# Moving the gate products, the key transposes and the score products to other places between the product groups of a fused attention and mixture-of-experts kernel

## The chip, the cores and the metric

The kernel runs on one core of a Trainium2 chip, as one launch. The metric is the time of that launch on the device, in microseconds. Each version is executed several times and the median counts. A profiled execution gives the trace from which the rows below come.

## The reference, cut to what matters

Three stages follow each other. Attention with 32 memory slots for each of 8 batches and 8 heads:

```python
a = softmax(phi, axis=seq)                       # 576 positions, 32 slots
k_m, v_m = a.T @ k, a.T @ v                      # per batch and head: 32 x 64
attn = softmax(scale * q @ k_m.T) @ v_m          # 576 x 64
x = attn, heads side by side                     # 4608 tokens x 512
```

Then a first feed-forward stage, `h = max(x @ w1, x @ w2, x @ w3)` (512 to 768) and `h @ w_out` (768 to 512). Then a second stage in which every token goes to the one of 8 experts with the highest `x @ w_gate`: `relu(x @ w1[e]) @ w2[e]`, times the gate's softmax value.

## The kernel before, in words

All products that carry precision are done as three products of split operands (`mm3`, L99 to L102: high by high, low by high, high by low). The kernel never forms the attention output. `u_step(b, f)` (L407) multiplies the memory values `vT` of batch b by the f-th 128 columns of the three first-stage weights, and splits the result into `u_hi` (ScalarE) and `u_lo` (VectorE). `m1_step` (L435) then multiplies u by the attention weights `at_hi`, `at_lo`. These 6 matmuls of 288 columns are one product group. The groups of one f come as two halves of the sequence by three weights (hf, i), so six groups use one u, and a batch has 36 groups. The first of three groups is copied out of PSUM by ScalarE into `hx` (L448). The second and third are folded into it by VectorE (`max`, L450), and after the third ScalarE and GpSimd make `h_hi` and `h_lo`. Then `m2_step` (L471) does the eight outputs of the batch by `wo_hi`, `wo_lo`.

PSUM has four tiles for product groups (`ps_mm`), two for u products (`ps_u`) and two for everything else (`ps_at`). `at_scores` takes both `ps_at` and both `ps_u` tiles. So TensorE can be at most four groups ahead of the engines that empty them.

Between the groups of batch b stand three other kinds of work. First, the attention of batch b + 1 (`attention`, L366): column maxima of phi, exponentials, `at_asum` (four VectorE operations), `at_km` (148 small products, L258), `at_kvT` (three transposes, L299, copied out as `kT` and `vT`), `at_scores` (64 products, L318, four VectorE transposes out of PSUM), then maxima, exponentials, sums and `at_out`. Second, the gate of batch b - 1: `gate_a` (16 products, L487), `gate_b` (five transposes and a chain of twelve small VectorE operations with one ScalarE exponential, L502, then a DMA issued by ScalarE), `gate_c` (two products and eight small VectorE operations, L535). Third, the u products: `u_step(b, 2)` to `u_step(b, 5)` are written in front of f = 1 to 4 of the same batch, and the first two u products of the next batch among its second-stage products.

Where the first two kinds go is set by a list of due times. A `Stream` holds (time, function) pairs, each product group advances its clock by 0.97, each second-stage step by 2.25, and whatever has come due is written then. `AT` (L56) is the list of the attention of batches 2 to 7, which are done in batches 1 to 6, the steady batches. Batch 1 has a list of its own, `AT1`. In the following, group n is the n-th product group of a batch. With these clocks the order before is: `gate_a` behind group 3, `gate_b` and the second u product (f = 2; counted here by its place, the first of the four in the batch) behind group 6, `gate_c` and the next u product (f = 3) behind group 12, `at_km` and u of f = 4 behind group 18, `at_kvT` behind group 19, `at_scores` behind group 22, u of f = 5 behind group 24.

TensorE's queue keeps this written order. The queues of VectorE and ScalarE don't: the framework's scheduler takes, for each engine, the earliest written operation that its own estimate calls ready, so later work can slip in front of earlier work that is still waiting. Once compiled, the order is fixed.

Of the kernel before, what the change touches and what calls it, by code (L numbers as in the profile page):

```python
# [19 lines left out]
def kernel(  # L20
# [32 lines left out]
    WARM = 17  # L53
    NRAW = 6

    AT = dict(max=1, col=4.5, sub=6.5, q=(0, 2, 3.5, 5), exp=9, asum=11, km=16.5, kvT=18, sc=20.5,  # L56
              smax=(24.5, 27), sexp=(29, 31), ssum=(34, 37), out=(41.5, 45))
    AT1 = dict(max=18, col=19, sub=20.5, q=(30, 31, 32, 33), exp=22, asum=23, km=31, kvT=33, sc=36,
               smax=(38, 39.5), sexp=(39.5, 41), ssum=(42, 44), out=(45, 47))
    XN = 256  # L60
# [65 lines left out]
    def load_phi(b, src=None):  # L126
        t = ep.tile([P, J, NCH, M], F32, tag="phi", name="phi_t")
        if src is not None:
            after(t[:, 0, 0, 0:1], src)
        nc.sync.dma_start(out=t.rearrange("p j c m -> p j (c m)"), in_=pairs(phi[b]))  # L130
        inp["phi", b] = t
# [234 lines left out]
    def attention(b):  # L366

        T = AT if b > 1 else AT1
        L = [
# [117 lines left out]
    def gate_a(b):  # L487
        gsb = mo["sy"].tile([P, S], F32, tag="gsb", name="gsb")
        st["gsb", b] = gsb
        for hf in range(2):  # L490
            ps = ps_at.tile([P, 512], F32, tag="at", name="ps_g")
            for d in range(ND):
                nc.tensor.matmul(
                    out=ps[32 * d:32 * d + 32, :HS],
                    lhsT=wg[:, d, :],
                    rhs=ys[b][:, d, hf * HS:(hf + 1) * HS],
                    start=True,
                    stop=True,
                )
            nc.scalar.activation(out=gsb[:, hf * HS:(hf + 1) * HS], in_=ps[:, :HS], func=AF.Copy)  # L500

    def gate_b(b):  # L502
        gsb = st.pop(("gsb", b))

        lg = rsmall.tile([P, NTT, E], F32, tag="glg", name="glg")
        for t0, t1 in ((0, 3), (3, NTT)):
            ps = ps_at.tile([P, 512], F32, tag="at", name="ps_l")
            for t in range(t0, t1):
                nc.tensor.transpose(ps[:, (t - t0) * P:(t - t0 + 1) * P], gsb[:, TT0[t]:TT0[t] + P], ident)
            nc.vector.tensor_reduce(  # L510
                out=lg[:, t0:t1],
                in_=ps[:, :(t1 - t0) * P].rearrange("p (t d e) -> p t e d", d=ND, e=32)[:, :, :E],
                axis=AX.X, op=ALU.add,
            )
        mx = rsmall.tile([P, NTT, 1], F32, tag="gmx", name="gmx")
        nc.vector.tensor_reduce(out=mx[:, :, 0], in_=lg, axis=AX.X, op=ALU.max)
        sh = rsmall.tile([P, NTT, E], F32, tag="gsh", name="gsh")
        nc.vector.tensor_tensor(out=sh, in0=lg, in1=mx.to_broadcast([P, NTT, E]), op=ALU.subtract)
        oh = rsmall.tile([P, NTT, E], F32, tag="goh", name="goh")
        nc.vector.scalar_tensor_tensor(out=oh, in0=sh, scalar=0.0, in1=w8, op0=ALU.is_ge, op1=ALU.mult)  # L520
        nc.scalar.activation(out=sh, in_=sh, func=AF.Exp)
        gt = gi[:, b, 0:NTT]
        ix = gi[:, b, NTT:2 * NTT]
        nc.vector.tensor_reduce(out=ix, in_=oh, axis=AX.X, op=ALU.max)
        nc.vector.tensor_tensor(out=oh, in0=w8, in1=ix.unsqueeze(2).to_broadcast([P, NTT, E]), op=ALU.is_equal)
        nc.vector.tensor_tensor(out=oh[:, NTT - 1], in0=oh[:, NTT - 1], in1=own, op=ALU.mult)
        oc = rsmall.tile([P, E], F32, tag="goc", name="goc")
        nc.vector.tensor_reduce(out=oc, in_=oh.rearrange("p t e -> p e t"), axis=AX.X, op=ALU.add)
        nc.vector.tensor_reduce(out=gt, in_=sh, axis=AX.X, op=ALU.add)
        nc.vector.tensor_scalar(out=gt, in0=gt, scalar1=EPS, scalar2=None, op0=ALU.add)  # L530
        nc.vector.reciprocal(out=gt, in_=gt)
        nc.scalar.dma_start(out=g_dram[b], in_=gi[:, b])
        st["goc", b] = oc

    def gate_c(b):  # L535
        oc = st.pop(("goc", b))
        ps = ps_at.tile([P, 512], F32, tag="at", name="ps_c")
        nc.tensor.matmul(out=ps[:, :E], lhsT=ones, rhs=oc, start=True, stop=True)
        cnt = rsmall.tile([P, E], F32, tag="cnt", name="cnt")
        nc.vector.tensor_copy(out=cnt, in_=ps[:, :E])  # L540
        cm = rsmall.tile([P, 1], F32, tag="cm", name="cm")
        nc.vector.tensor_reduce(out=cm, in_=cnt, axis=AX.X, op=ALU.max)
        ce = rsmall.tile([P, E], F32, tag="ce", name="ce")
        nc.vector.scalar_tensor_tensor(out=ce, in0=cnt, scalar=cm, in1=w8[:, 0], op0=ALU.is_equal, op1=ALU.mult)
        nc.vector.tensor_reduce(out=cm, in_=ce, axis=AX.X, op=ALU.max)

        nc.vector.scalar_tensor_tensor(
            out=scal[:, b], in0=gi[:, b, NTT:2 * NTT], scalar=cm, in1=gi[:, b, 0:NTT], op0=ALU.is_equal, op1=ALU.mult
        )

        nc.vector.tensor_scalar(out=ce, in0=w8[:, 0], scalar1=cm, scalar2=None, op0=ALU.not_equal)
        nc.vector.tensor_tensor(out=rest[:, b], in0=cnt, in1=ce, op=ALU.mult)
        nc.vector.tensor_scalar(out=e1i[0:1, b:b + 1], in0=cm[0:1], scalar1=-1.0, scalar2=float(E), op0=ALU.mult, op1=ALU.add)
# [264 lines left out]
    with ExitStack():  # L818
# [65 lines left out]
        def start_step():  # L884
            if started[0] < len(wparts):
                w_done(started[0], scored if started[0] < 8 else None)
                started[0] += 1

        for b in range(B):
            stream = Stream(attention(b + 1) if b + 1 < B else [])  # L890
            if b > 0:
                stream.add([(2, lambda: gate_a(b - 1)), (5, lambda: gate_b(b - 1)), (11.5, lambda: gate_c(b - 1))])
            else:
                done = lambda n: wdst[n][0:1, 0:1]
                stream.add([(10, lambda: load_phi(1, done(10)))])
                stream.add([(16 + i, lambda i=i: load_kv(1, i, done(13))) for i in range(2)])
                stream.add([(20 + j, lambda j=j: load_q(1, j, done(15))) for j in range(J)])
            for f in range(NF1):
                if f + 1 < NF1 and b > 0 and f > 0:
                    u_step(b, f + 1)  # L900
                if (b, f) == (B - 1, NF1 - 2):
                    early.close()
                    mo["stack"] = ExitStack()
                    mo["xp", 0] = mo["stack"].enter_context(tc.tile_pool(name="xp", bufs=1, side="right"))
                    feed = Feed(
                        [(c, 0, i) for c in "y12" for i in range(ND)]
                        + [(c, n, i) for n in range(1, B) for c in "y12" for i in range(ND)]
                        + [("1", B, i) for i in range(ND)]
                    )
                    feed.load_to(feed.AHEAD)  # L910
                    stream.add([(1 + 1.7 * i, feed.step) for i in range(3 * ND)])
                for hf in range(2):
                    for i in range(3):
                        m1_step(b, f, hf, i)
                        if b == 0 and (hf, i) in ((0, 0), (0, 2), (1, 1)):
                            start_step()
                        if b == 0 and 0 < f < NF1 - 1 and (hf, i) == (1, 0):
                            u_step(0, f + 1)
                        stream.advance(0.97)
            if b == 0:  # L920
                while started[0] < len(wparts):
                    start_step()
                start.close()
                mo["sy"] = late.enter_context(tc.tile_pool(name="sy", bufs=1))
            for hf in range(2):
                if b == 0 and hf == 0:
                    m2_by_f(b, hf, stream)
                    continue
                for d in range(ND):
                    m2_step(b, d, hf)  # L930
                    stream.advance(2.25)
                    if b + 1 < B and (hf, d) in (((0, 2), (1, 1)) if b else ((1, 0), (1, 1))):
                        u_step(b + 1, int((hf, d) == (1, 1)))
            stream.rest()
# [46 lines left out]
        for b in range(B):  # L981
            stream = Stream([])
# [75 lines left out]
```

## Time and profile before

| | us |
|---|---|
| median of 3 runs | 1015.35 |
| lowest and highest run | 1012.68, 1017.62 |
| the profiled execution's own time | 1014.16 |
| its span, first to last instruction | 1012.4 |

Some 2 us of the execution lie outside the span. Times in the rows are microseconds from the start of the span. In a timeline row the columns are start, duration, engine, line, operation, output and inputs, shape, count of merged instructions, and in brackets how long the engine had been idle and what ended that. PE is TensorE's matmuls, PEld its weight loads, DVE VectorE, ACT ScalarE, ACTq ScalarE's queue when it issues a DMA. Matmuls are pipelined, so the start of one to the start of the next is the time that counts.

### The profile page before, as it was taken

What the parts mean: (1) busy time and instruction counts of PE and PEld (TensorE: products, weight loads), DVE (VectorE), ACT (ScalarE), POOL (GpSimd) and SP (SyncE); (2) the same over time, 40 slices, a digit from 0 to 9 for tenths busy, and PEclk for the clock granted to TensorE, in tenths of its full rate; (3) what the DMA queues carried; (4) which work ended last, traced back from release to release, by engine and by line L of the source; (5) the groups of instructions that cost most, each with busy time, mean ns of one, the idle gap of its engine ahead of it and who ended that gap; (6) DMA issues with size and microseconds to landing.
All of it is one profiled execution on the core that took longest, in us unless ns stands there. A gap on an engine that the chain in (4) does not pass through costs nothing. (4 is left out here: it accounts for less than half of the span.)

```text
span 1012.4 us, 20551 instructions
## 1 busy us (share of the span) xinstructions
PE 978.7 (97%) x8306; PEld 854.6 (84%) x8306; DVE 562.1 (56%) x1289; ACT 370.5 (37%) x808; POOL 149.9 (15%) x259
## 2 busy tenths in 40 slices
PE   7888999999999999999999999999999999999996
PEld 4466788879888898988989989898989898989885
DVE  6889877473674737657165727171717171716341
ACT  2555343333433324334245415050506060604130
POOL 0000012110211102112021130202021212121110
PEclk9899999999999999999999999999999999999999
DMA  8487423132221322110117417171717161615030
GB/s 288 135 259 262 141 66 103 47 130 83 75 92 48 131 83 75 46 47 2 48 61 251 164 40 221 35 226 32 229 32 228 33 212 49 211 45 151 22 110 22
DMA packets 59107, 114.79 MB, mean 113 GB/s; under 512 B 7687, under 2 KB 20999, under 8 KB 59008
## 3 DMA queue, kind: packets, MB, share of 16 engines
q1 hardware_dynamic: 48480, 94.01, 28.5%
q0 software_dynamic: 4768, 9.94, 4.2%
q10 hardware_dynamic: 5760, 9.48, 2.5%
q8 instruction: 67, 1.10, 0.5%
q14 instruction: 32, 0.26, 0.1%
HBM read 94.00 MB, written 19.44 MB: 112 GB/s over the span
## 5 line engine op out<-in xcount | busy, mean ns | idle before, releaser
L100 PE MATMUL ps_m<-at_hi,u_hi 128*128 128x288 f32 x576 | 177.9, 310 | 6.9 <-ACT hx L448 3.2
L102 PE MATMUL ps_m<-at_hi,u_lo 128*128 128x288 f32 x576 | 170.5, 297 | 0.2 <-ACT u_lo L427 0.2
L101 PE MATMUL ps_m<-at_lo,u_hi 128*128 128x288 f32 x576 | 170.3, 296 | 0.1
L100 PE MATMUL ps_x<-yh,w1h 128*128 128x288 f32 (+1 forms) x544 | 160.3, 295 | 0.2 <-DVE xh L617 0.2
L101 PE MATMUL ps_x<-yl,w1h 128*128 128x288 f32 (+1 forms) x544 | 159.9, 294 | 0.0
L102 PE MATMUL ps_x<-yh,w1l 128*128 128x288 f32 (+1 forms) x544 | 159.8, 294 | 0.0
L97 POOL TENSOR_TENSOR h_lo<-hx,h_hi 128x288 fp32r<-128x288 f32 x84 | 72.9, 868 | 466.3 <-ACT h_hi L96 462.3
L100 PEld LDWEIGHTS ps_m<-at_hi,u_hi 128*128 128x128 f32 x576 | 108.2, 189 | 37.3 <-issue 14.2
L646 POOL DMA_DIRECT2D out_dram<-o x144 | 71.1, 500 | 346.2 <-DVE o L643 306.0
L450 DVE TENSOR_TENSOR hx<-hx,ps_m 128x288 f32<-128x288 f32 x192 | 85.5, 448 | 65.2 <-PE ps_m L102 40.9
L100 PE MATMUL ps_m<-h_hi,wo_hi 128*128 128x288 f32 x384 | 115.1, 300 | 1.9 <-DVE hx L450 1.8
L101 PE MATMUL ps_m<-h_lo,wo_hi 128*128 128x288 f32 x384 | 113.2, 295 | 0.0
L102 PE MATMUL ps_m<-h_hi,wo_lo 128*128 128x288 f32 x384 | 113.0, 295 | 0.0
L102 PEld LDWEIGHTS ps_m<-at_hi,u_lo 128*128 128x128 f32 x576 | 108.7, 189 | 1.4 <-ACT u_lo L427 0.7
L101 PEld LDWEIGHTS ps_m<-at_lo,u_hi 128*128 128x128 f32 x576 | 108.7, 189 | 1.2 <-issue 1.0
L643 DVE TENSOR_SCALAR o<-ps_x,scal 128x512 f32<-128x512 f32 x32 | 24.0, 751 | 151.6 <-PE ps_x L102 151.6
L100 PE MATMUL ps_x<-w2h,xh 128*128 128x512 f32 x272 | 107.7, 396 | 0.0
L101 PE MATMUL ps_x<-w2l,xh 128*128 128x512 f32 x272 | 107.5, 395 | 0.0
L102 PE MATMUL ps_x<-w2h,xh 128*128 128x512 f32 x272 | 107.4, 395 | 0.0
L100 PEld LDWEIGHTS ps_x<-yh,w1h 128*128 128x128 f32 x544 | 102.3, 188 | 1.5 <-DVE xh L617 0.5
L101 PEld LDWEIGHTS ps_x<-yl,w1h 128*128 128x128 f32 x544 | 102.1, 188 | 0.6 <-ACT yl L732 0.2
L102 PEld LDWEIGHTS ps_x<-yh,w1l 128*128 128x128 f32 x544 | 102.1, 188 | 0.0
(200 smaller groups left out, 1593.6 us busy)
## 6 DMA issues: line engine op xcount, KB each, us to landing
raw<-in_moe_w_dram SPq DMA_DIRECT2D x72, 512.0 KB, 4.7
raw<-y_dram SPq DMA_DIRECT2D x36, 288.0 KB, 3.1
w<-in_moe_w_dram SPq DMA_DIRECT2D x18, 512.0 KB, 5.1
kv_t<-in_k_dram SPq DMA_DIRECT2D x8, 1152.0 KB, 7.1
kv_t<-in_v_dram SPq DMA_DIRECT2D x8, 1152.0 KB, 9.8
q_t<-in_q_dram SPq DMA_DIRECT2D x32, 288.0 KB, 3.0
y_dram<-y_sb ACTq DMA_DIRECT2D x32, 288.0 KB, 2.1
out_dram<-o POOLq DMA_DIRECT2D x144, 64.0 KB, 1.9
```

Source lines behind the costliest of these rows:

```text
L97: eng.tensor_tensor(out=dst_lo, in0=src, in1=dst_hi, op=ALU.subtract)
L100: nc.tensor.matmul(out=ps, lhsT=hi_l, rhs=hi_r, start=first, stop=False)
L101: nc.tensor.matmul(out=ps, lhsT=hi_l, rhs=lo_r, start=False, stop=False)
L102: nc.tensor.matmul(out=ps, lhsT=lo_l, rhs=hi_r, start=False, stop=last)
L450: nc.vector.tensor_tensor(out=hx[0], in0=hx[0], in1=ps, op=ALU.max)
L643: nc.vector.tensor_scalar(out=o, in0=ps, scalar1=scal[:, b, t:t + 1], scalar2=None, op0=ALU.mult)
L646: nc.gpsimd.dma_start(out=out5[b, half, c], in_=o[i:i + TB])
```

## The change

It moves work between the product groups of the steady batches, and the gate's work also in batch 7. Nothing is added or removed, and no size changes.

```diff
-    AT = dict(..., km=16.5, kvT=18, sc=20.5,
-              smax=(24.5, 27), sexp=(29, 31), ssum=(34, 37), out=(41.5, 45))
+    AT = dict(..., km=16.5, kvT=23.2, sc=25.5,
+              smax=(29.5, 31.5), sexp=(33.5, 35.5), ssum=(38, 40.5), out=(44, 47))
...
-                stream.add([(2, lambda: gate_a(b - 1)), (5, lambda: gate_b(b - 1)), (11.5, lambda: gate_c(b - 1))])
+                stream.add([(5.7, lambda: gate_a(b - 1)), (11.5, lambda: gate_b(b - 1)), (23.1, lambda: gate_c(b - 1))])
```

By the clocks the new order is: `gate_a` and u of f = 2 behind group 6, `gate_b` and u of f = 3 behind group 12, `at_km` and u of f = 4 behind group 18 as before, `gate_c`, `at_kvT` and u of f = 5 behind group 24, `at_scores` behind group 27. The softmax of the scores is written later too: its last step, `at_out` for the second half, behind the sixth of the eight second-stage steps in place of the fifth. The loads of the next batch's phi, k and v are written with `at_kvT`.

## Rows read from the trace of the kernel before

**Rows 1.** The page: busy time of TensorE and others over the span.
```profile
PE 978.7 (97%) x8306; PEld 854.6 (84%) x8306; DVE 562.1 (56%) x1289; ACT 370.5 (37%) x808; POOL 149.9 (15%) x259
```
**Rows 2.** Windows view: busy time and instructions by engine, then PEclk, granted clock.
```profile
193.43:204.89 11.46, 11.36 (x103) 9.60 (x101) 10.89 (x35) 5.25 (x13) 2.52 (x3) 1.00 0.01 0
```
**Rows 3.** Waits from 125 to 500 us: total, times, longest.
```profile
PEld ps_u L414 <- DVE sc L335: 5.8, 12, 1.1
```
**Rows 4.** Timeline of PE in batch 2, around u of f = 5.
```profile
217.20 0.29 PE L102 MATMUL ps_m<-at_hi,u_lo 128*128 128x288 f32 x1
218.32 1.24 PE L414 MATMUL ps_u<-w,vT 64*32 64x384 f32 x16 [0.83 <-DVE sc L335]
219.49 0.40 PE L100 MATMUL ps_m<-at_hi,u_hi 128*128 128x288 f32 x1
```
**Rows 5.** Timeline of PE in batch 2, u of f = 4.
```profile
209.60 0.88 PE L414 MATMUL ps_u<-w,vT 64*32 64x384 f32 x16
210.40 0.40 PE L100 MATMUL ps_m<-at_hi,u_hi 128*128 128x288 f32 x1
210.64 0.29 PE L101 MATMUL ps_m<-at_lo,u_hi 128*128 128x288 f32 x1
```
**Rows 6.** Timeline of PE in batch 2, around gate_a.
```profile
188.92 0.29 PE L102 MATMUL ps_m<-at_hi,u_lo 128*128 128x288 f32 x1
189.14 1.18 PE L493 MATMUL ps_g<-y_sb,wg 128*32 128x288 f32 x16
190.25 0.40 PE L100 MATMUL ps_m<-at_hi,u_hi 128*128 128x288 f32 x1
```
**Rows 7.** Timeline of PE in batch 2, from u of f = 2 to group 18.
```profile
193.50 0.88 PE L414 MATMUL ps_u<-w,vT 64*32 64x384 f32 x16
...
198.37 0.29 PE L102 MATMUL ps_m<-at_hi,u_lo 128*128 128x288 f32 x1
198.76 0.41 PE L100 MATMUL ps_m<-at_hi,u_hi 128*128 128x288 f32 x1
...
199.89 0.88 PE L414 MATMUL ps_u<-w,vT 64*32 64x384 f32 x16
...
204.51 0.29 PE L101 MATMUL ps_m<-at_lo,u_hi 128*128 128x288 f32 x1
204.64 0.29 PE L102 MATMUL ps_m<-at_hi,u_lo 128*128 128x288 f32 x1
204.93 0.40 PE L100 MATMUL ps_m<-at_hi,u_hi 128*128 128x288 f32 x1
```
**Rows 8.** Timeline of DVE in batch 2, the same stretch and u of f = 4.
```profile
193.43 0.40 DVE L510 TENSOR_REDUCE glg<-ps_l 128x24 f32<-128x96 f32 x2
...
196.10 0.98 DVE L97 TENSOR_TENSOR u_lo<-ps_u,u_hi 128x384 fp32r<-128x384 f32 x2
196.99 1.35 DVE L243 TENSOR_TENSOR phi_t<-phi_t,ps_mb 128x1152 f32<-128x1152 f32 x1
198.26 1.59 DVE L450 TENSOR_TENSOR hx<-hx,ps_m 128x288 f32<-128x288 f32 x3
199.96 0.69 DVE L217 TENSOR_TENSOR hc<-phi_t 128x512 f32<-128x512 f32 x1
...
201.52 0.15 DVE L540 COPY cnt<-ps_c 128x8 f32<-128x8 f32 x1
...
203.57 0.21 DVE L547 SCALAR_TENSOR_TENSOR scal<-gi,cm 128x5 f32<-128x5 f32 x1
...
204.44 0.99 DVE L450 TENSOR_TENSOR hx<-hx,ps_m 128x288 f32<-128x288 f32 x2
...
211.60 1.02 DVE L97 TENSOR_TENSOR u_lo<-ps_u,u_hi 128x384 fp32r<-128x384 f32 x2 [1.48 <-ACT u_hi L96]
```
**Rows 9.** Timeline of ACT in batch 2, behind gate_b.
```profile
196.21 0.34 ACTq L532 DMA_DIRECT2D g_dram<-gi  x1
196.65 0.41 ACT L448 ACTIVATE hx<-ps_m 128x288 f32<-128x288 f32 x1 [0.46 <-DVE u_lo L97]
```

More of the change, by code (lines that the diff above doesn't have):

```diff
@@ L54 @@
     NRAW = 6
-    AT = dict(max=1, col=4.5, sub=6.5, q=(0, 2, 3.5, 5), exp=9, asum=11, km=16.5, kvT=18, sc=20.5,
-              smax=(24.5, 27), sexp=(29, 31), ssum=(34, 37), out=(41.5, 45))
+    AT = dict(max=1, col=4.5, sub=6.5, q=(0, 2, 3.5, 5), exp=9, asum=11, km=16.5, kvT=23.2, sc=25.5,
+              smax=(29.5, 31.5), sexp=(33.5, 35.5), ssum=(38, 40.5), out=(44, 47))
     AT1 = dict(max=18, col=19, sub=20.5, q=(30, 31, 32, 33), exp=22, asum=23, km=31, kvT=33, sc=36,
```

## The prediction, made before the change was run

> **What bounds the kernel now.** I read the page first. TensorE is busy for 97% of the span [rows 1], so nothing else can shorten the time much: only idle time of TensorE, pauses between its products, or product work. The change alters no product work, so what is left is idle time and pauses in the steady batches. I looked for them in the list of waits, cut to those batches, and then in TensorE's timeline of batch 2, by the distance from one start to the next. Inside a run of group products that distance is 0.13 us (204.51 to 204.64) [rows 7].
>
> The list of waits has one entry that the change can touch directly: the weight loads of u products waited 5.8 us in all for the VectorE transposes of the scores, twelve times, two per steady batch [rows 3]. The timeline shows the place. The scores take both u tiles behind group 22, and u of f = 5 stands only two groups behind them. In batch 2 the last group product starts at 217.20, the u product at 218.32, the next group at 219.49 [rows 4]. The same u product with nothing in its way takes 0.80 (209.60 to 210.40) [rows 5], and an ordinary entry into other work takes 0.22 (188.92 to 189.14) [rows 6]. So here 2.29 - 0.80 - 0.22 = 1.27 us is lost.
>
> Two smaller stalls stand where TensorE has filled all four group tiles and waits for VectorE. The first is at group 12: 0.39 in place of 0.13, so 0.26 (198.37 to 198.76). The second is at group 18: 0.29, so 0.16 (204.64 to 204.93) [rows 7]. After any pause the first spacing is 0.24 (210.40 to 210.64), 0.11 more than usual [rows 5]. So they cost 0.37 and 0.27. Their reason is VectorE's backlog. From gate_b's first operation to the end of group 18's stall, VectorE is busy for 10.89 of 11.46 us, at a granted TensorE clock of 1.00, the 2.4 GHz level [rows 2]. In that stretch it runs gate_b, u_lo, the subtraction from phi, three hx operations in one piece from 198.26, then asum and gate_c [rows 8].
>
> **The change part by part.** There are six steady batches, 1 to 6. The gate moves in batch 7 too.
>
> *u of f = 5 goes ahead of the scores.* No scores are in its tiles any more, so the wait of 5.8 us goes. What stays of it is the ordinary entry into a u product, 0.22 - 0.13 = 0.09 per batch, 0.5 in all. I take a gain of 5.3, with 4.8 and 5.8 as bounds; 1.27 in batch 2 is above the mean of 0.97.
>
> *Fewer breaks.* gate_a's 16 products take 1.11 wherever they are (189.14 to 190.25) [rows 6]. Joined to a u product they save one slow first spacing, 0.11 [rows 5], in seven batches: 0.8. The key transposes, joined to gate_c and u, save as much in six batches, 0.7, unless the switch from one kind of product to the next costs it back. The trace has no such triple, so I take half of it. Together 1.1, with 0.3 and 1.5 as bounds.
>
> *gate_b leaves u of f = 2.* gate_b takes VectorE from 193.43 to 196.10, 2.67 us, and u_lo, phi and three hx wait behind it [rows 8]. Without it the stall at group 12 goes: 0.37 per batch. How much sooner does the work behind it start? At u of f = 4 u_lo starts 2.0 after its product (209.60 to 211.60) [rows 5, 8]. At u of f = 2 that would be 195.5 in place of 196.10 [rows 7, 8], so the subtraction, the exponentials and asum come 0.6 sooner.
>
> *gate_b arrives at u of f = 3, where asum already is, and gate_c leaves it.* gate_c is eight operations of about 0.15 to 0.21 [rows 8], some 1.4 us, so VectorE's pile there grows by 2.67 - 1.4, about 1.3. Behind it stand the hx operations of groups 14 and 15, and behind these TensorE at group 18. In strict order: asum starts at 199.96 - 0.6 = 199.36; to the first hx it was 204.44 - 199.96 = 4.48 and is now 5.8; with the hx (0.99 for two) group 14's tile is free at 205.65. TensorE would like to start group 18 at 204.93 - 0.16 - 0.37 = 204.40. It would stall 1.25 in place of 0.16, a loss of 1.1 against the 0.37 from group 12: 0.7 per batch, 4.3 over six. At the other end hx of group 14 is let in between the steps of gate_b's chain, as gate_c's steps now alternate with other operations between 201.52 and 203.57 [rows 8]. Then both stalls go, 0.64 per batch, 3.8 over six. The pile has enough other operations (asum, u_lo) to fill the first gaps of the chain, but not all. I am between the ends and take 0.
>
> The Trainium skill, in the page "PSUM — Partial Sum Buffer", section "Engine vs sequencer instructions", says that VectorE's queue is strictly first in, first out. The trace agrees: the two hx operations at 204.44 run as one piece of 0.99 us, so the second had been waiting with its input there [rows 8]. The rule speaks against this change: once compiled behind gate_b, an hx can't pass it, and the time would be that of the second rival below.
>
> *gate_c arrives at u of f = 5, and the scores follow three groups later.* Now the scores wait for the u tiles. From the start of u to the scores there are 0.80, 18 spacings of 0.13 and one slow one: 3.3 us. At u of f = 4 u_lo ended 3.02 after its product's start (209.60, 211.60 + 1.02) [rows 5, 8]. That is 0.3 to spare. gate_c's 1.4 us come in front of u_lo, but its input is there before u starts, so most of them fall in the 2.0 us in which u_lo has to wait anyway. I take 0.1 per batch, 0.6 in all. The bounds are nothing, and 1.4 - 0.3 = 1.1 per batch, 6.6, if all of gate_c delays u_lo.
>
> *The softmax of the scores moves back five groups.* I cost it at nothing. The cover is the second stage of the batch, eight steps of 18 products at 0.13, 19 us, in which VectorE's queue has no hx. If that cover were gone, the first group of the next batch would wait for `at_lo`. The loads written with `at_kvT` go through a queue with nothing in front of them, and their data is wanted in the next batch only.
>
> Sum: 5.3 + 1.1 + 0 - 0.6 = 5.8 us. Against the profiled execution, 1014.16, that is 1008.4. The median of the runs shown, 1015.35, is 1.2 us above it, and I leave the forecast at 1008.4. The least difference that a measurement of this kernel can tell from none is about 0.5%, 5.1 us.
>
> **The rivals.** *The pile doesn't form.* VectorE's work spreads out, and groups 12 and 18 no longer stall. For it: gate_b goes away from the phi subtraction, and total VectorE work is the same. Time: 1008.4 - 3.8 = 1004.6.
>
> *The pile stands in strict order*, as worked out above. For it: VectorE is 95% busy there already [rows 2]. Against it: steps of a chain now do alternate with other work. Time: 1008.4 + 4.3 = 1012.7.
>
> *The wait only moves*, so that the change doesn't do what it says: the scores wait for u_lo as long as u waited for the scores. Against it: 0.3 us to spare and gate_c's early input. Time: 1008.4 - 0.6 + 6.6 = 1014.4, no change.
>
> *Slower: ScalarE holds the pile.* gate_b ends in a DMA issue on ScalarE, 0.34, and the hx copy behind it, 0.41, waits [rows 9]. At u of f = 2 this is harmless. At u of f = 3 gate_b's chain ends later, and if group 13's copy is queued behind the issue, the order is: asum and an hx (4.48 less 1.0 of u_lo and 1.4 of gate_c, 2.1), gate_b 2.67, u_lo 1.0, from 199.36 to 205.1; the issue and the copy to 205.9; hx of group 14 to 206.4. Against 204.40 that is a stall of 2.0, a loss of 1.84 - 0.37 = 1.5 per batch, 8.8 over six. Time: 1008.4 + 8.8 = 1017.2, slower than before. It decides from a loss of 1.0 per batch on (5.8 / 6). Against it: the scheduler puts the copy first if it thinks that gate_b is late.
>
> **How the numbers follow.** My case has a chance of 0.50 with a range of its own of 1006 to 1011. The pile that doesn't form has 0.17, the strict pile 0.18, the moved wait 0.08, ScalarE's hold 0.07. Faster than 1009.1 (0.5%) are some 0.31 of my case and all of the first rival: 0.48. Slower than 1019.2 is only the far end of the last rival with the scatter of the runs, which reach from 1012.68 to 1017.62: 0.05. Within 0.5% stays 0.47. The range of 8 in 10 reaches from 1003.5, just past the first rival, to 1015.0, which takes in the strict pile and the moved wait and leaves out ScalarE's hold and the tails.
>
> **What would show it right or wrong.** Right: no wait of u products for the scores' transposes in the list of waits; u of f = 5 takes 0.80 to the next product; the scores enter in about 0.2; TensorE's start of group 12 comes without a pause. To be looked at first: the start of group 18 against 0.13, and what VectorE runs between u of f = 3 and hx of group 14. A pause of 1 us or more there in every steady batch means the strict pile; a pause in front of the ninth score product means the moved wait; a late hx copy of group 13 on ScalarE means the last rival. A pause in front of a batch's first group would mean that the cover of the late softmax was too short, and the prediction wrong in a step that I cost at nothing.

## The result, and the profile after

The changed kernel took 1000.61 us, median of 4 runs (999.66 to 1001.2), against 1014.01 us of the kernel before, run beside it (4 runs, 1008.65 to 1017.62): a ratio of 0.986, interval 0.9833 to 0.9888. A second copy of it, timed another time, took 1002.18 against 1013.19 (0.9894, 0.9861 to 0.9927). So the change gains 11 to 13.4 us; forecast were 5.8, with 1003.5 as the low end. The prediction was wrong in size and right in sign.

The profiled execution took 999.66 us with a span of 997.9. The page's line of TensorE and the others has the same share as before [rows 1], with 8 us less of busy time:

```profile
PE 970.4 (97%) x8306; PEld 850.7 (85%) x8306; DVE 565.3 (57%) x1289; ACT 375.0 (38%) x808; POOL 148.0 (15%) x259
```

In the list of waits of the steady batches (125 to 495 us) the weight loads of u products no longer wait for the transposes of the scores [rows 3]. In its place stands a small wait of the scores for the low half of u:

```profile
PEld ps_sc L327 <- DVE u_lo L97: 0.8, 3, 0.3
```

TensorE's timeline of batch 2, from u of f = 2 to behind the scores, in the order of time:

```profile
189.07 0.88 PE L414 MATMUL ps_u<-w,vT 64*32 64x384 f32 x16
...
193.93 0.30 PE L102 MATMUL ps_m<-at_hi,u_lo 128*128 128x288 f32 x1
194.06 0.29 PE L100 MATMUL ps_m<-at_hi,u_hi 128*128 128x288 f32 x1
...
194.86 0.71 PE L509 MATMUL ps_l<-ident,gsb 128*128 128x128 f32 x5
195.50 0.88 PE L414 MATMUL ps_u<-w,vT 64*32 64x384 f32 x16
...
200.25 0.30 PE L102 MATMUL ps_m<-at_hi,u_lo 128*128 128x288 f32 x1
200.39 0.29 PE L100 MATMUL ps_m<-at_hi,u_hi 128*128 128x288 f32 x1
...
209.94 0.28 PE L538 MATMUL ps_c<-goc,ones 128*128 128x8 f32 x2
210.08 0.42 PE L303 MATMUL ps_kvT<-ident,kx 128*128 128x128 f32 x2
...
210.54 0.88 PE L414 MATMUL ps_u<-w,vT 64*32 64x384 f32 x16
211.34 0.40 PE L100 MATMUL ps_m<-at_hi,u_hi 128*128 128x288 f32 x1
...
213.91 1.60 PE L327 MATMUL ps_sc<-qT,kT 32*32 32x288 f32 x64
215.44 0.40 PE L100 MATMUL ps_m<-at_hi,u_hi 128*128 128x288 f32 x1
```

Group 12 starts 0.13 behind the product ahead of it and group 18 0.14 (200.25 to 200.39): both pauses of before, 0.26 and 0.16 [rows 7], are gone. u of f = 5 takes 0.80 to the next product, as an undisturbed one does [rows 5], where it took 1.17 [rows 4].

I summed all distances between products over the six steady batches, from the first product of batch 1 to the first of batch 7: 375.29 us before, 364.98 after, 10.3 less. The terms are these. u of f = 5: its entries took 4.82 us in all where the ordinary ones are 6 x 0.22, and it ran 6 x 0.36 too long, so 3.50 + 2.16 = 5.66, all gone. The pauses at groups 12 and 18: 1.57 + 1.01 = 2.58, gone. Slow first spacings in the product groups: their excess falls from 6.6 to 4.2, so 2.4, of which 12 x 0.11 = 1.3 belong to those two pauses. The scores, from the start of the first of the 64 products to the start of the last, summed over the six batches: 7.21 before, which is 1.20 each, and 8.12 after, a loss of 0.91. (This is how "the scores took" is meant from here on; to the next group it is 0.33 more.) Together 5.66 + 2.58 + 2.4 - 0.91 = 9.7. The other 0.6 are single pauses, which fall from 3.0 to 2.1 and for which the profile shows no releaser, less some 0.3 that the new switches between kinds of products cost.

The other 4.2 us between the two profiled executions (14.5 in all) lie almost wholly where both kernels have the same instructions in the same order: 1.7 in the expert stage, 1.4 ahead of the first group, 0.8 in batch 0. Batch 7, whose gate work moved too, has 0.2. The before profile has a visible piece of it, a stretch late in the expert stage at the 1.2 GHz level. This is its windows view; the column before the last two is the granted clock:

```profile
974.00:976.70 2.70, 2.08 (x19) 2.09 (x19) 2.64 (x3) 2.68 (x6) 0.00 (x0) 1.00 0.69 266
976.70:980.10 3.40, 3.40 (x18) 3.40 (x18) 2.40 (x8) 0.74 (x3) 0.99 (x2) 0.50 0.17 41
```

TensorE was busy for 2.08 of the 2.70 us ahead of the fall. The profile after has no such stretch there.

### The profile page after: what moved, and what is told of

It reads as the page before. It is cut to its first block, busy times and chain, and to the rows that moved or that the text cites. A ratio compares the mean times of both kernels' runs of the same rounds, so it can differ in the third digit from the quotient of the medians.

```text
span 997.9 us, 20544 instructions
## 1 busy us (share of the span) xinstructions
PE 970.4 (97%) x8306; PEld 850.7 (85%) x8306; DVE 565.3 (57%) x1289; ACT 375.0 (38%) x808; POOL 148.0 (15%) x259
## 5 line engine op out<-in xcount | busy, mean ns | idle before, releaser
L100 PE MATMUL ps_m<-at_hi,u_hi 128*128 128x288 f32 x576 | 174.9, 305 | 4.8 <-ACT hx L448 2.3
```

Source lines behind the costliest of these rows:

```text
L100: nc.tensor.matmul(out=ps, lhsT=hi_l, rhs=hi_r, start=first, stop=False)
```

## The experiments

In what follows "steady" is the distance just used, from the first product of batch 1 to the first of batch 7. It is compared with 375.29 and 374.31 of two profiles of the kernel before, mean 374.80, and with 364.98 and 365.56 of two of the changed kernel, mean 365.27. Two profiles of one kernel differ by 0.6 to 1.6 us in it (three kernels here were profiled twice), so a difference of 2 us counts, where the launch time needs 5.

### The two kernels once more

A copy of the kernel before, and one of the changed kernel.

> The kernel before, unchanged, to see what differs from one execution to the next. In the two profiles at hand the steady batches (start of batch 1 to start of batch 7) took 375.3 us before and 365.0 after, a difference of 10.3, and the remaining 4.2 of the 14.5 us stood in batch 0 and in the expert stage, where the instructions are the same. Theory: those 4.2 us are scatter, so this run shows 374 to 377 in the steady batches and differs by 1 to 4 us from the first profile elsewhere. Rival: the change acts on those stages too, and this run repeats the first profile there within 0.5 us.

> The changed kernel, unchanged, on the same chip as the next three. Theory: the steady batches again take 364 to 366 us against 374 to 375, and whatever the whole time gains beyond these 10 us is scatter of batch 0 and the expert stage, so the whole time comes out some 11 us under the kernel before, at 1002 to 1005. Rival (the change acts on the other stages too): 1000 to 1001 again, and the expert stage at 447.6 or less against 449.3 and 452.0 in the two profiles of the kernel before.

The first took 1015.31 us against 1015.28 (ratio 1.0004, 0.9977 to 1.0031), the second is in the result above. The gain in the steady batches repeats (365.56). In this second profile the scores took 9.37 us in all, 2.74 of them in batch 2, where `u_lo` ended late.

### Half of the change each

First the scores and the softmax as changed, the key transposes and the gate as before:

```diff
-    AT = dict(..., kvT=18, sc=20.5, smax=(24.5, 27), ...
+    AT = dict(..., kvT=18, sc=25.5, smax=(29.5, 31.5), ...
```

> The scores and the softmax behind them at their new places, key transposes and gate at the old. Theory (three terms that add): only the wait of u of f = 5 goes, worth 5.6 us less up to 0.9 for a pause of the scores; the stalls at groups 12 and 18 stay at 0.26 and 0.16 us. Steady batches 370 to 371 us, whole time some 5 us under the kernel before. Rival (the scores carry the whole gain, since VectorE's backlog comes from them): steady batches at 365 to 367 and no stall at group 12.

It took 1004.95 us (0.9896, 0.9864 to 0.9929), steady 368.56. u of f = 5 was entered in 0.22 and took 0.80, the scores took 1.20 in every batch, and the pauses of 0.27 at group 12 and 0.16 at group 18 stayed. This half is worth 374.80 - 368.56 = 6.2 us.

Then the gate as changed and the attention as before:

```diff
-(2, lambda: gate_a(b - 1)), (5, lambda: gate_b(b - 1)), (11.5, lambda: gate_c(b - 1))
+(5.7, lambda: gate_a(b - 1)), (11.5, lambda: gate_b(b - 1)), (23.1, lambda: gate_c(b - 1))
```

> The gate's three pieces at their new places, key transposes and scores at the old. Theory (three terms that add): the stalls at groups 12 and 18 go, 0.64 us per steady batch or 3.8, and one slow first spacing per batch, 0.7 in all; the wait of u of f = 5 stays at about 0.9 per batch. Steady batches 370 to 371 us, whole time some 4.5 us under the kernel before. Rival (the pile as forecast): the stall at group 18 grows to 1 us and the steady batches stay at 375 or rise.

It took 1005.95 us (0.9911, 0.9883 to 0.9938), steady 367.53. No pause stands at groups 12 and 18. Here is its list of waits, at the wait that the scores' half removes:

```profile
PEld ps_u L414 <- DVE sc L335: 3.0, 10, 0.5
```

That is 2.8 us less than in [rows 3]. The products of `gate_c`, now ahead of u of f = 5, fill part of the time for which u had to wait, 0.16 per batch or 1.0 in all; why the rest is shorter stays open. So this half gains 7.3 by itself, and the two do not add up to the whole: 6.2 + 7.3 = 13.5, against 9.5 together. What the gate is worth in the complete change is what it adds to the first half, with the joined key transposes and less the wait of the scores that `gate_c` brings: 368.56 - 365.27 = 3.3 us. My sum had nothing for `gate_b`, and 0.11 per batch for `gate_a`.

The joined key transposes alone were undone too (`kvT=18` in the changed kernel).

> The changed kernel with the key transposes back behind group 19, alone. Theory (joining them is worth nothing: in the changed kernel gate_c and the transposes take 0.60 us together, in the kernel before 0.21 and 0.25 with a slow first spacing of 0.1): steady batches within 0.5 us of the changed kernel, or up to 0.9 shorter if the copies of kT and vT on ScalarE had delayed the u tiles for the scores. Rival (each break costs an entry, an exit and a slow spacing, 0.3 us): steady batches 1.5 to 2 us longer.

It took 1001.02 us (0.9873, 0.9838 to 0.9907), the same as the changed kernel. There is no profile of it from which the stages could be read, so only the time speaks: joining them is worth nothing that can be measured.

### Is it the place of gate_a and gate_b?

The changed kernel with these two parts back in their old places:

```diff
-(5.7, lambda: gate_a(b - 1)), (11.5, lambda: gate_b(b - 1)), (23.1, ...
+(2, lambda: gate_a(b - 1)), (5, lambda: gate_b(b - 1)), (23.1, ...
```

> The changed kernel with the first two parts of the gate where they were before (2 and 5), the third part, the key transposes and the scores as changed. Theory: the VectorE pile of before comes back in u of f=2 (the second part of the gate beside the low half that GpSimd takes), and with it the pause of 0.26 us at group 12 and its slow spacing of some 0.1 us in each of the six steady batches, and the pause at group 18 stays away because the third part is no longer queued at group 12: steady 367 to 368.5 us. Rival: the pause at group 12 comes from the third part that followed there, and then it is gone here too: steady 365 to 366.

Steady was 368.83, 3.6 more than the changed kernel; the one time was 1009.07. Its TensorE timeline in batch 2, at group 12:

```profile
198.10 0.29 PE L102 MATMUL ps_m<-at_hi,u_lo 128*128 128x288 f32 x1
198.49 0.40 PE L100 MATMUL ps_m<-at_hi,u_hi 128*128 128x288 f32 x1
198.73 0.29 PE L101 MATMUL ps_m<-at_lo,u_hi 128*128 128x288 f32 x1
```

The 0.39 and the slow 0.24 of before are back [rows 7, 5], in each of the six batches, and group 18 has no pause. So the stall at group 12 belongs to `gate_b` in u of f = 2 (`gate_a` went back with it, but has no VectorE operation). The one at group 18 belongs to `gate_c` in u of f = 3: it stays in the run with the scores alone moved, where `gate_c` is in its old place, and is gone here. Both leave with their part of the gate. The rival fell.

### How much room the pile has left

The changed kernel with more VectorE work behind `gate_b`, two passes over the gate's input in batches 1 to 6:

```diff
+        if b < B - 2:
+            for _ in range(2):
+                nc.vector.tensor_scalar(out=gsb, in0=gsb, scalar1=1.0, scalar2=None, op0=ALU.mult)
```

> The changed kernel with two VectorE operations of 576 columns added behind gate_b in batches 1 to 6; they rewrite a gate buffer with itself and are there for their time alone, some 0.9 us. Theory (the pile at u of f = 3 stays just 0.2 us under what four group tiles cover): a pause of 0.5 to 0.8 us at group 18 and a slow first spacing of 0.1 behind it, 3 to 5 us over six batches, steady batches 368 to 370. Rival (hx gets in between the steps of the chain, so length does not matter): no pause, steady batches at 365.

It took 1003.5 us (0.9905, 0.9873 to 0.9938), steady 365.66. In TensorE's timeline group 18 now starts 0.31 behind the last product, and in VectorE's the work that it waits for is this:

```profile
203.56 0.29 PE L102 MATMUL ps_m<-at_hi,u_lo 128*128 128x288 f32 x1
203.87 0.40 PE L100 MATMUL ps_m<-at_hi,u_hi 128*128 128x288 f32 x1
```

```profile
203.30 0.18 DVE L531 RECIPROCAL gi<-gi 128x5 f32<-128x5 f32 x1
203.40 0.41 DVE L450 TENSOR_TENSOR hx<-hx,ps_m 128x288 f32<-128x288 f32 x1
```

The pause is 0.18 us, in all six batches. 0.90 us more work made the `hx` of group 14 end only 0.31 later (5.01 us behind the start of u of f = 3, 4.70 in the changed kernel), since the rest went into gaps of the chain. The truth lay between the two theories. The changed kernel has no stall here, but has only 0.2 us to spare. Steady doesn't show the cost of 6 x 0.29 = 1.7 us, since the scores waited less here (7.66 in all) and such a sum is close to what two profiles differ by.

The other way to fill the pile is `gate_c` behind `gate_b` at once (11.6 in place of 23.1).

> The changed kernel with gate_c back behind group 12, right behind gate_b, so that VectorE has asum, gate_b and gate_c there. In the changed kernel the hx of group 14 ends 0.2 us before TensorE wants its tile for group 18, and gate_c took 0.95 us from start to start before. Theory (the pile is real and the change merely stays 0.2 us under it): a stall of 0.7 to 0.9 us at group 18 in each steady batch, steady batches 369 to 371 us. Rival (the hx gets in between the steps of the chains however long they are): no stall, steady batches at 365.

It took 1012.77 us (0.9973, 0.9953 to 0.9993), steady 373.31: the whole gain of the gate and more was gone, but not by the stall that I expected. This is its wait list for TensorE, and the place in batch 2:

```profile
PE ps_c L538 <- DVE gi L530: 7.4, 6, 1.2
```

```profile
199.53 0.29 PE L100 MATMUL ps_m<-at_hi,u_hi 128*128 128x288 f32 x1
201.06 0.36 PE L538 MATMUL ps_c<-goc,ones 128*128 128x8 f32 x2 [1.24 <-DVE gi L530]
```

The product of `gate_c` reads `goc`, near the end of `gate_b`'s chain; it stood in TensorE's queue 1.4 us too early, and all groups stood behind it. The run says nothing about VectorE's pile.

### Why gate_b was so long in its old place

In VectorE's and GpSimd's timelines of the kernel before, in batch 2, one operation of `gate_b` stands out:

```profile
194.07 0.80 POOL L97 TENSOR_TENSOR h_lo<-hx,h_hi 128x288 fp32r<-128x288 f32 x1 [2.93 <-ACT h_hi L96]
```

```profile
194.10 0.83 DVE L518 TENSOR_TENSOR gsh<-glg,gmx 128x40 f32<-128x40 f32 x1
```

40 columns take 0.83 us, and they end just behind the `h_lo` that GpSimd makes at the time. The view of that tile gives the eight instances of each kernel as least, median and longest duration in ns. Before, after, and (below) the kernel before with `h_lo` on VectorE:

```profile
L518 DVE TENSOR_TENSOR gsh<-glg,gmx x8: 199/829/832, 131.9 to 558.0; 128x40 f32<-128x40 f32 x8
```

```profile
L518 DVE TENSOR_TENSOR gsh<-glg,gmx x8: 199/201/826, 137.0 to 545.3; 128x40 f32<-128x40 f32 x8
```

```profile
L518 DVE TENSOR_TENSOR gsh<-glg,gmx x8: 192/195/201, 130.2 to 550.2; 128x40 f32<-128x40 f32 x8
```

Seven of eight are long before, one of eight after. The experiment took GpSimd out of it, with the gate in its old place:

```diff
-            split(hs[b, f][0][:, sl], hs[b, f][1][:, sl], hx[0], nc.gpsimd if b else nc.vector)
+            split(hs[b, f][0][:, sl], hs[b, f][1][:, sl], hx[0], nc.vector)
```

> The kernel before with the low half of h always taken on VectorE, none on GpSimd. Theory: VectorE operations with both inputs in SBUF take three to four times as long while GpSimd takes that low half (0.83 against 0.20 us for the gate's scaling, 0.90 against 0.29 for the sum of the attention maxima, in this kernel's own traces), because the two engines share their way into SBUF: here the gate's scaling takes 0.20, the attention sum 0.29 and the maximum 0.29 us in all batches. Rival: they are long for what stands ahead of them in VectorE's own queue or for their place in the batch, and keep 0.8 to 0.9 us. VectorE gets some 0.45 us more per low half, so the time itself is no better than before by either.

> The kernel before with the low half of h on VectorE, as in the one look before, timed against the kernel before. Theory (the pile of before comes from GpSimd slowing VectorE): the pauses at groups 12 and 18 are gone again although VectorE has 0.45 us more work per half of h; the wait at u of f=5 stays at 0.4 to 1.3 us, as it comes from the transposes of the scores; steady batches 370 to 371 us as in the one look (370.21) against 375.29 and 374.31 of the kernel before, and the time 3.5 to 5 us shorter, ratio 0.995 to 0.9965. Rival: the one look had a favourable execution (its time was 1012.69 beside a median of 1012.99), the ratio is 0.999 to 1.002.

Two profiles have steady at 370.21 and 368.63, 4.6 and 6.2 less than before. The timed copy took 1008.03 us (0.9929, 0.9906 to 0.9953), a larger gain than the theory had; the first one was executed once, in 1012.69. `gsh` takes 0.20 in all eight batches, and every `asum` and `mx` 0.29. In the second profile's VectorE timeline of batch 2:

```profile
190.28 0.40 DVE L510 TENSOR_REDUCE glg<-ps_l 128x24 f32<-128x96 f32 x2
...
190.87 0.46 DVE L97 TENSOR_TENSOR h_lo<-hx,h_hi 128x288 fp32r<-128x288 f32 x1
191.25 0.20 DVE L518 TENSOR_TENSOR gsh<-glg,gmx 128x40 f32<-128x40 f32 x1
...
192.62 0.98 DVE L97 TENSOR_TENSOR u_lo<-ps_u,u_hi 128x384 fp32r<-128x384 f32 x2
```

`u_lo` starts 2.34 us behind `gate_b`'s first operation, 0.33 earlier than in [rows 8], though VectorE now does `h_lo` between the two. And TensorE enters group 12 like this:

```profile
195.22 0.29 PE L102 MATMUL ps_m<-at_hi,u_lo 128*128 128x288 f32 x1
195.35 0.34 PE L100 MATMUL ps_m<-at_hi,u_hi 128*128 128x288 f32 x1
```

0.13, without a pause; the pause at group 18 is gone too. So more work for VectorE removed VectorE's pile, because it removed what slowed VectorE down. At group 12 the experiment leaves no other reason: VectorE's operations from `gate_b` to the `hx` that TensorE waits for stand in the same order as before, with `h_lo` put in. At group 18 the compiled order changed as well, with the `hx` of group 14 now ahead of the last four steps of `gate_c`, so how much of that pause went with GpSimd is not shown. The second part of my rival, that the time would be no better, failed with it. A part of the 6.2 us isn't the pile: this profile's wait of u of f = 5 was 1.5 us shorter than that of before (4.3 in the list of waits, against 5.8).

The cross test is the same edit in the changed kernel.

> The changed kernel with the low half of h on VectorE. Theory: the changed kernel has no pile left at groups 12 and 18, so what the low half on VectorE can still give is the third part of the gate without its collision (its last product is some 0.4 us shorter) and so the 0.2 to 0.4 us that the scores wait in batches 1, 3 and 5; against it stand two times 0.45 us more of VectorE per f: steady batches 364 to 365.5 us, ratio to the kernel before 0.987 to 0.990, like the changed kernel's. So taking GpSimd out is worth some 4 us in the kernel before and less than 1 here, since the change has already taken the gate out of GpSimd's way. Rival: the gain of the low half is separate from that of the gate's place, and steady falls by 3 us or more, to 362 or less.

It took 1000.83 us (0.988, 0.9854 to 0.9905), steady 364.26, and the scores took 1.20 in all six batches. So taking `h_lo` from GpSimd is worth some 5 us in the kernel before and 1 in the changed one, no more than two profiles of one kernel differ by. That is what one expects if the new place of the gate has already taken `gate_b` out of GpSimd's way.

### Scores nearer to u, and farther

The scores one group behind u of f = 5 in place of three (`sc=23.9`):

> The changed kernel with the scores one group behind u of f = 5 in place of three. In the changed kernel u_lo of that product ended 3.2 us after the product's start in batch 2, and the scores started 3.4 after. Theory (the wait moves to the scores when they stand too close): the scores take 2.6 to 2.9 us to the next group in place of 1.53, 5 to 7 us over six batches, steady batches 370 to 372. Rival (the tiles come free earlier, because VectorE's queue is arranged anew): scores at 1.5 to 1.9, steady batches at 365.

It took 1014.55 us (0.9994, 0.997 to 1.0018), steady 377.51. Its list of waits:

```profile
PEld ps_sc L327 <- DVE u_lo L97: 8.5, 12, 1.4
```

The wait has moved, to the place that the rival of the moved wait named. The scores took 3.38, 3.48, 3.36, 2.31, 2.90 and 2.15 us. I had expected less. Of the 12.2 us by which steady is longer than in the changed kernel, 8.8 are these waits (17.58 in all, against 8.12 and 9.37). Most of the rest is TensorE's clock: this is the only profile with stretches at the 1.2 GHz level in the steady batches, from 157.0 to 160.4 and from 221.9 to 225.3 us, at a granted clock of 0.51. Each comes right behind the scores, where TensorE had been busy for 6.19 of 7.04 and 6.67 of 7.92 us, and in each the group products follow at 0.24 in place of 0.13, some 1.5 us lost. So the distance of three groups is what the scores' half of the change rests on: at one group the waits cost more than the 6.2 us that this half gives.

Three groups farther (`sc=26.5`), first together with a moved transpose of the phi maximum (`col=5.6`), then alone:

> The changed kernel with the scores behind group 28 instead of group 25 (sc=26.5), and with the transpose of the phi maximum beside the gate's product behind group 6 (col=5.6) instead of behind group 4. Theory: in the changed kernel the 64 score products took 1.60, 1.20, 1.54, 1.20, 1.38 and 1.20 us in batches 1 to 6, so three of them still wait 0.2 to 0.4 us; three more groups later none waits (1.20 each, 0.9 us less in sum), and one switch fewer per batch takes some 0.1 us: steady batches 363.3 to 364.3 us against 364.98 and 365.56 in the two profiles of the changed kernel, time 999 to 1001. Rival: the scores of queries and keys are needed in time by their maxima, so putting them later only moves the 0.2 to 0.4 us to the products of the attention's output, and the phi chain now starts 0.3 us per group later and lets the u groups wait: steady 365 to 367.

> The changed kernel with the scores behind group 28 alone (sc=26.5), the transpose of the phi maximum where the change has it. Theory: of the run with both, the later scores gained (the 64 products took 1.20 us in five batches of six) and the transpose cost (it put the gate's 16 products in two halves with two u products between, 0.6 to 0.8 us per batch); so this run has scores of 1.20 us in at least five batches, no new pause, and steady batches of 363.5 to 365 us, ratio 0.987 to 0.989. Rival: the later scores let the attention's output wait, and steady is 366 or more.

The first took 1006.43 us (0.9924, 0.9899 to 0.9949), steady 369.64. The scores took 1.20 in five batches of six, but this is TensorE's timeline at the moved transpose:

```profile
188.32 0.69 PE L493 MATMUL ps_g<-y_sb,wg 128*32 128x288 f32 x8
188.94 0.83 PE L414 MATMUL ps_u<-w,vT 64*32 64x384 f32 x2
189.70 0.69 PE L493 MATMUL ps_g<-y_sb,wg 128*32 128x288 f32 x8
190.33 0.87 PE L414 MATMUL ps_u<-w,vT 64*32 64x384 f32 x14
191.12 0.40 PE L100 MATMUL ps_m<-at_hi,u_hi 128*128 128x288 f32 x1
```

The compiled order was now mixed: two u products stand between the halves of the gate's products. So TensorE's queue does not always keep the written order, as I said of it ahead of the prediction. From the first gate product to the next group it is 2.80 us where the changed kernel needs 1.91 (1.11 + 0.80). That is 0.9 per batch, more than the later scores gave. The second run, without this, took 1000.79 us (0.9879, 0.9849 to 0.9908), steady 364.05, scores 7.71 in all. It is 1.2 us better in steady and not to be told from the changed kernel in time.

The last run put `gate_c` beside the key means at group 18 (17.4 in place of 23.1).

> The changed kernel with the third part of the gate behind group 18 (17.4), beside the key means, instead of behind group 24. Theory: VectorE's queue ahead of the score transposes then holds no gate work in u of f=5, so the low half of q is written earlier and the scores take 1.20 us in every batch (the changed kernel: 1.60, 1.54 and 1.38 in batches 1, 3 and 5): 0.9 us less in sum; group 18 already breaks the stream for the key means, so the product of the gate there costs no new switch (0.1 us per batch less): steady 363.5 to 364.5 us. Rival: at group 18 the product of the gate finds the column that VectorE writes in the second part not long done, and TensorE waits there as in the run with this part right behind the second (up to 1.5 us per batch): steady 366 to 374.

It took 1005.41 us (0.9912, 0.9887 to 0.9937), steady 369.96, 4.7 more than the changed kernel. The scores were 1.20 in every batch, as the theory said, but the compiled order put `gate_c`'s products inside the u products again, and there they waited 0.22 us for a `ps_at` tile:

```profile
208.23 0.84 PE L414 MATMUL ps_u<-w,vT 64*32 64x384 f32 x4
209.29 0.39 PE L538 MATMUL ps_c<-goc,ones 128*128 128x8 f32 x2 [0.22 <-ACT vx L297]
209.61 0.86 PE L414 MATMUL ps_u<-w,vT 64*32 64x384 f32 x12
```

None of the versions tried beats the changed kernel by more than can be measured.

## Why the prediction was wrong, point by point

*u of f = 5 ahead of the scores: right.* Taken 5.3 with 4.8 to 5.8 as bounds, measured 5.66 as idle time, and 6.2 for the run with this half alone.

*The scores wait for the u tiles: right.* Taken 0.6, with 0 to 6.6 as bounds; measured 0.91 in one profile and 2.2 in the other (9.37 - 7.21). The run with the scores close by shows that the bound was real.

*Fewer breaks: near enough.* Taken 1.1, with 0.3 and 1.5 as bounds. The slow first spacings that don't belong to the two pauses fall by 2.4 - 1.3 = 1.1, and the new switches cost some 0.3. `gate_a` beside u saves one slow first spacing of 0.11 in a batch. The key transposes save another, but leaving them for u takes 0.20 where leaving them for a group took 0.03, so nothing can be measured of them.

*gate_b's old and new place: this step failed.* The prediction put the two ends at -4.3 and +3.8 and said: "I am between the ends and take 0." By its number the upper end came true. The two pauses and their slow spacings, 2.58 + 1.3 = 3.9, went and nothing came in their place; by runs, the gate's parts are worth 3.3 to 3.6. With 3.8 in place of 0 the sum for the steady batches is 9.6, and measured are 9.5 (374.80 - 365.27). That these agree to 0.1 is partly luck: u of f = 5 gave 0.4 to 0.6 more than taken, the scores waited 0.3 to 1.6 more, and single pauses added 0.4 to 0.9.

The upper end's reason, that the `hx` of group 14 is let in between the steps of `gate_b`'s chain, is hardly why it came true. This is VectorE's timeline of the changed kernel, batch 2:

```profile
190.56 1.02 DVE L97 TENSOR_TENSOR u_lo<-ps_u,u_hi 128x384 fp32r<-128x384 f32 x2 [2.04 <-ACT u_hi L96]
191.50 1.35 DVE L243 TENSOR_TENSOR phi_t<-phi_t,ps_mb 128x1152 f32<-128x1152 f32 x1
...
194.70 0.68 DVE L217 TENSOR_TENSOR hc<-phi_t 128x512 f32<-128x512 f32 x1
...
196.25 0.25 DVE L510 TENSOR_REDUCE glg<-ps_l 128x24 f32<-128x96 f32 x1
196.42 0.84 DVE L219 TENSOR_TENSOR asum<-hc,phi_t 128x128 f32<-128x128 f32 x1
...
197.73 0.20 DVE L518 TENSOR_TENSOR gsh<-glg,gmx 128x40 f32<-128x40 f32 x1
...
199.69 0.16 DVE L530 TENSOR_SCALAR gi<-gi 128x5 f32<-128x5 f32 x1
199.75 0.45 DVE L450 TENSOR_TENSOR hx<-hx,ps_m 128x288 f32<-128x288 f32 x1
200.12 0.18 DVE L531 RECIPROCAL gi<-gi 128x5 f32<-128x5 f32 x1
```

The `hx` of group 14 at 199.75 stands behind eleven of the twelve operations of `gate_b`; only the reciprocal comes after it. So the order was nearly the strict one, and what failed is the price of that order. The prediction put the end of this `hx` at 205.65 - (199.89 - 0.37) = 6.13 us behind the start of u of f = 3, with 4.88 as the limit (204.40 less the same 199.52). It came at 4.70 or 4.71 in all six batches of both profiles, 0.2 us before TensorE started group 18. The 1.43 us between are made up as follows.

First, 0.64 is the start of the pile. `hc`, the first step of the attention sum, starts 0.80 ahead of u of f = 3 (194.70, and 195.50 in TensorE's timeline), where the sum had it 0.16 ahead (199.36 and 199.52). Of this 0.41 is TensorE's own time, which I had left out: the five transposes of `gate_b` now stand in front of u of f = 3, in place of the two products of `gate_c`, so that u starts 6.43 behind u of f = 2 (189.07 to 195.50) and not 6.02. The other 0.23 is VectorE's: `hc` starts 5.63 behind u of f = 2 where it started 6.46 behind it [rows 7, 8], so 0.83 sooner and not 0.6. `u_lo` followed its product after 1.49 and not after the 2.0 that I took from another f.

Second, 0.79 is the length of the pile, from `hc` to the end of that `hx`: 5.50 in place of 6.29 (205.65 - 199.36). `gate_b` is not 2.67 us of VectorE wherever it stands. 0.63 of that was `gsh` held up by GpSimd, and in the new place `gsh` takes 0.20; with its steps between others, the eleven ahead of the `hx` took 1.61 us of VectorE from start to start. `gate_c`, which left, had taken 0.95 so counted, not 1.4. So the pile from `hc` to the start of the `hx` grew by 0.57 (4.48 to 5.05) and not by 1.3. I read the length of `gate_b` off [rows 8] from its first start to the start of what followed, and did not look at its single operations, where one of 40 columns at 0.83 beside others at 0.20 would have shown it.

The rival of the strict pile fell by its price and not by its order. The rule of the Trainium skill cited ahead of it is not contradicted: the queue ran in its compiled order, and no `hx` passed a step that stood in front of it. ScalarE's hold did not come either: with the pauses gone there is no late copy to price. The late softmax did cost nothing: no first group of a batch has a pause in front of it.

*What the sum could not hold.* 9.5 of the 11 to 13.4 us are in the steady batches. With the right value for `gate_b`, 1014.16 - 9.6 = 1004.6, the forecast of the first rival, would still be 2.4 to 4 us above the runs, though inside the range; the wrong step and this rest together took the result out of it. The rest lies almost wholly in stages whose instructions did not change. The record gives the mean granted clock of every run. Over 74 runs of the kernel before, from 1008.9 to 1018.7 us, it is 0.9886 on average, and the longer the time, the lower the clock (correlation -0.83). Over the eight runs of the changed kernel it is 0.9909. The 0.0023 between are 2.3 us of 1000, an estimate for a kernel that TensorE bounds: so much of the rest goes with less time at the 1.2 GHz level. One place of it is the stretch at 1.2 GHz in the expert stage: 6 of 16 profiles have one, and their expert stage (from its first product to its last) takes 449.3 to 452.9 us, while the 10 without take 446.8 to 448.9. Three of the four profiles with the old order of gate and scores have it, and none of the four with the changed order and nothing else but the later scores or the low half on VectorE. Why the changed kernel spends less time at this level, and whether the change makes it so, stays open; no run was made for it.

## What to carry to other kernels

Before a group of small operations is priced for a new place, look at its single operations in the old one: an operation that is four times as long as its neighbours of the same size may be held up by something that stays behind when it moves. Work for an idle engine is not free if that engine slows the one it should relieve: here giving VectorE back its 0.45 us per half removed a VectorE backlog. And a consumer of tiles that another engine has to empty needs a distance in TensorE's own work (here three groups, 18 products); with one group the wait came back whole, and two were not tried. Last, work that moves on one engine moves the others' starts too: here five transposes that went with `gate_b` gave VectorE 0.41 us.

## What the runs showed of the hardware

*VectorE beside GpSimd.* Small VectorE operations with both inputs in SBUF that started while GpSimd made `h_lo` took about three to four times as long: `gsh` 0.83 against 0.20 us, the third step of `asum` 0.90 against 0.29, one step of `mx` 0.84 against 0.29, `scal` 0.61 against 0.22. Operations with an input in PSUM did not: `hx` took 0.45 with and without overlap, `u_lo` 0.55. With no `h_lo` on GpSimd all of them were short in every batch. The Trainium skill has this in the page "SBUF — State Buffer", section "Who interferes with whom": a VectorE instruction with two SBUF inputs and a GpSimd instruction that reads SBUF exclude each other, and the one that comes second waits for the whole of the other. The trace agrees in the main: `gsh` started at 194.10, 0.03 behind `h_lo`, and ended 0.06 behind it; and in the changed kernel an `h_lo` that started at 194.98, during `hc`, took 1.07 in place of 0.80. It ended 0.67 behind `hc`, so it had not waited for quite the whole of it. The rule, beside the 0.80 us of `h_lo`, would have pointed at the price of the old place ahead of time.

*The switch of products.* A u group split by other products pays its entry and exit twice: 0.9 us per batch where the gate's products were mixed into it, as shown above.

*Clock.* The granted clock fell to the 1.2 GHz level for some us late in the expert stage in 6 of 16 profiles, in the one shown after a stretch with 0.62 us of idle TensorE in 2.70. With the scores one group behind u it fell twice in the steady batches too, right behind the waits of the scores.
